# One written list of steps for the first attention, scores of two heads in one matmul, and weight conversion without GpSimd

## The chip, the cores and the metric

The kernel runs on one NeuronCore of one Trainium2 chip, in a single launch. A core has TensorE (PE in the profile; PEld is its weight load), VectorE (DVE), ScalarE (ACT), GpSimd (POOL) and SyncE (SP), each with an instruction queue of its own, and 16 DMA engines. The metric is device microseconds of one execution. Three runs of the kernel before took 930.74, 930.91 and 933.34 us; their median is 930.91 us.

## The reference

Two stages, for 8 batches of 576 rows. First an attention of 8 heads with 64 columns each, masked (heads 0 to 3 see the last 32 keys, heads 4 to 7 every 32nd key), then a mixing of rows and two large products:

```python
scores = scale * np.matmul(q, k.transpose(0, 1, 3, 2))
scores = np.where(masks[None, :, :, :], scores, -1000000000.0)
attn = np.exp(scores - np.max(scores, axis=-1, keepdims=True))
attn = attn / (np.sum(attn, axis=-1, keepdims=True) + 1e-09)
x = np.matmul(attn, v)            # heads side by side: (8, 576, 512)
h = x.transpose(0, 2, 1) @ U @ V  # U: 576 x 32, V: 32 x 576
u = x + h.transpose(0, 2, 1)
out = u + np.maximum(u @ w_ch1, 0.0) @ w_ch2   # 512 x 2048, 2048 x 512
```

q, k and v are float32; U, V, w_ch1 and w_ch2 come as float64, and the device turns them to float32 itself.

## The kernel before, in words

**Products.** The rows are cut into 9 blocks of 512 (8 batches' first 512 rows, and one block of what is left). For each block, `gemm1` makes 16 tiles of 128 hidden columns (12 matmuls each: 4 pieces of 128 inner rows, three products of high and low parts), and `gemm2` adds each into four accumulators (12 more). `gemm2` of a tile comes two tiles after its `gemm1` (`LAG`).

**Weights.** They arrive as 32 raw chunks of 128x512 float64, in the order of `CHUNK_SEQ`. `conversion` turns a chunk into high and low parts: two ACT instructions and two of DVE (`to_f32`), a copy on ACT into `parts[:, 0]`, and a subtraction on GpSimd (line 150) into `parts[:, 1]`. `gemm1` of the first tile needs the first four chunks.

**The first attention.** Batch 0 (strided heads as windows of reordered rows) is done before the first product. It is four pairs of heads: `scores` (two mask matmuls, then 36 small float32 ones, one for each 32 rows and head), `shifted` (maximum and subtraction on DVE), `exponentials` (ACT), `transposed` (five PE transposes), `to_sbuf` (ACT), `outputs` (36 small matmuls against the values and a column of ones), `normalised` (DVE). Then `mix_t` (x by U, for the strided and the local half), `u_strided_early` and `u_local` (transposes of x plus h, split into high and low parts `uh`, `ul`). The generators of the pairs are run three steps apart, and a scheduler that works with modelled times sets each engine's order there; the conversions of U, V and the first five chunks are held back behind an exponential by `gate`.

**The first block.** From the first product on, each engine's instructions stand in written order (`InOrder`). An agenda sets conversions, batch 1's attention ("second pairs") and the rest between halves of `gemm1` and `gemm2`, by ticks; 27 conversions start two ticks apart. In the later blocks the local heads go through `attention_pair`, and the strided heads of batches 2 to 7 run on GpSimd and DVE.

**DMA.** All transfers are issued by SP: keys, queries and values of pair 0, masks, the identity, pairs 2 and 3, U, V, pair 1, then 14 weight chunks.

All instructions of PE, DVE and ACT are issued in one helper, so they carry its line: L64 before and L69 after; DMAs are L86 and L92.

Of the kernel before, what the change touches and what calls it, by code (L numbers as in the profile page):

```python
# [19 lines left out]
NCH = S // 32  # L20
# [9 lines left out]
STAGGER = 3  # L30
ATT_BUFS = 7
PAIR_ORDER = (0, 2, 3, 1)
# [5 lines left out]
CHUNK_ORDER = (2, 3, 0, 1)  # L38


@with_exitstack
def fused_kernel(ctx, tc, lqk, lv, eqk, ev, sqkv, U, V, wts, masks, eye, out):
# [10 lines left out]
    class InOrder:  # L53
        on = False
# [15 lines left out]
    tensor, vector, scalar = InOrder(nc.tensor), InOrder(nc.vector), InOrder(nc.scalar)  # L70
# [12 lines left out]
    last_dma, gate, exps = [None], [], []  # L83

    def dma(out, in_):
        last_dma[0] = nc.sync.dma_start(out=out, in_=in_).ins  # L86
# [3 lines left out]
    masks_sb = const.tile([128, 768], BF16, name="masks_sb")  # L90
# [14 lines left out]
    def to_f32(raw, p, n, steps=1, gated=True):  # L105
# [5 lines left out]
        with tc.issue_after(gate[0]) if gated and gate else nullcontext():  # L111
            scalar.activation(out=f, in_=hi_w.bitcast(F32), func=AF.Abs, scale=2.0 ** -112)
            scalar.activation(out=low, in_=octet, func=AF.Copy, scale=1 / 32, bias=-15.5 / 32)
        yield steps
# [3 lines left out]
        vector.scalar_tensor_tensor(out=i, in0=i, scalar=3, in1=low, op0=ALU.logical_shift_left, op1=ALU.bitwise_or)  # L118
        yield steps
# [11 lines left out]
    def load_weights(n):  # L131
        while wl["loaded"] < min(n, len(chunks)):
            k = wl["loaded"]
            c = chunks[k]
            raws[c] = const.tile([128, 512], I64, name="raw%d_%d_%d" % c, tag=wtag(*c))
            with tc.issue_after(last_dma[0]):
                dma(out=raws[c], in_=wts[k])
            wl["loaded"] += 1

    def conversion(gated=False):  # L140
# [4 lines left out]
        f = yield from to_f32(raws[c], 128, 512, gated=gated)  # L145
        yield 1
# [3 lines left out]
        nc.gpsimd.tensor_tensor(out=parts[:, 1], in0=f, in1=parts[:, 0].bitcast(F32), op=ALU.subtract)  # L150

    def convert(n):
        while wl["conv"] < n:
            finished(conversion(True))
# [4 lines left out]
    raw_u = att([128, 320], "raw_u", I64)  # L159
    raw_v = ap_.tile([32, S], I64, name="raw_v", tag="vt")  # L160

    def small_loads():
        dma(out=raw_u, in_=U)
        dma(out=raw_v, in_=V)

    def small_u():
        f = finished(to_f32(raw_u, 128, 320))
        vector.tensor_copy(out=U_sb.rearrange("p v t r -> p (v t r)"), in_=f)

    def small_v():  # L170
        f = finished(to_f32(raw_v, 32, S))
        scalar.copy(out=Vst[0:32], in_=f)
        scalar.copy(out=Vst[32:64], in_=f)
        vector.tensor_tensor(out=Vst[64:96], in0=f, in1=Vst[0:32].bitcast(F32), op=ALU.subtract)
        nc.gpsimd.tensor_copy(out=Vp.rearrange("p (r i) -> p r i", i=NCH),
                              in_=Vst.bitcast(F32).rearrange("p (i r) -> p r i", r=32))
# [16 lines left out]

    def shifted(sp):
# [7 lines left out]
    def exponentials(s_sb):  # L202
        exped = scalar.activation(out=s_sb, in_=s_sb, func=AF.Exp, scale=0.125)
        if banks["prefix"]:
            exps.append(exped.ins)
            gate[:] = [exped.ins]
# [14 lines left out]
    def outputs(PT, vt):  # L221
        op = psx2()
        for c in range(NCH):
            t, c4 = c // 4, c % 4
            for hh, rows in enumerate(halves):
                tensor.matmul(op[32 * c4:32 * c4 + 32, hh, (D + 1) * t:(D + 1) * t + D + 1], PT[rows, 32 * c:32 * c + 32],
                                 vt(c)[rows], start=True, stop=True, skip_group_check=True,
# [3 lines left out]
    def normalised(op, pr):  # L231
        rt = ap_.tile([128, 16], F32, name="rt", bufs=2)[:, 0:10].rearrange("p (h t) -> p h t", h=2)
        for rows, ts in ((slice(0, 128), slice(0, 4)), (slice(0, 64), slice(4, 5))):
            o, r = op[rows, :, ts], rt[rows, :, ts]
            vector.tensor_scalar(out=r, in0=o[..., D], scalar1=1e-9, scalar2=None, op0=ALU.add)
            vector.reciprocal(out=r, in_=r)
# [125 lines left out]
    def mix_steps(b, half):  # L362
# [5 lines left out]
        for j in range(4):  # L368
            part = slice(64 * j, 64 * j + 64)
            tensor.matmul(ps_a[32 * j:32 * j + 32, part], U_sb[:, uv, 4, :], x[:, 4, part], start=False, stop=True,  # L370
# [12 lines left out]
        copied = scalar.copy(out=dst[64:96], in_=ta)  # L383
        if banks["prefix"]:
            gate[:] = [copied.ins]
        yield 1
        vector.tensor_tensor(out=dst[32:64], in0=ta, in1=dst[0:32].bitcast(F32), op=ALU.subtract)
# [12 lines left out]
    def split_steps(n, dcs, src, engine, order=None):  # L400
# [3 lines left out]
        scalar.copy(out=uh, in_=src)  # L404
        yield 1
# [17 lines left out]
    def u_local_steps(b, dcs):  # L423
        px = psx2()
        for dc in dcs:
            ps = px[:, dc % 2]
            for t in range(4):
                tensor.matmul(ps[:, 128 * t:128 * t + 128], x_loc[:, t, 128 * dc:128 * dc + 128], ident,
                                 is_transpose=True, start=t == 0, stop=False, skip_group_check=True)
            mixed(ps, b, dc, Vst, 0, TB, False)  # L430
# [15 lines left out]
    def u_strided_early_steps(b, dc):  # L446
        px = psx2().rearrange("p a x -> p (a x)")
        for t in range(5):
# [3 lines left out]
                             start=t in (0, 4), stop=False, skip_group_check=True)  # L452
        mixed(px[:, 0:512], b, dc, Vp, 0, 512, False)
# [3 lines left out]
        scalar.copy(out=tail_of(b)[:, dc].rearrange("p (i r) -> p r i", r=32), in_=src[:, :, 16:NCH])  # L457
        yield from split_steps(b, dc, src[:, :, 0:16], vector, "p (i r) -> p r i")
# [137 lines left out]
    def first_attention():  # L596
        late = [const.tile([128, 9, D + 1], F32, name=f"ve{n}", tag=wtag(n // 4, 3, n % 4)) for n in range(8)]
        loads = {}

        def load(k):  # L600
            pr = PAIR_ORDER[k]
            if k < 3:
                qk = places[2 * k:2 * k + 2]
            else:
                qk = [att([128, S], "kT"), att([128, S], "qT")]
# [33 lines left out]
        for dc in range(2):  # L639
            u_local(0, (dc,))  # L640
# [237 lines left out]
```

## Time and profile before

| what | value |
|---|---|
| three runs, median | 930.91 us (930.74 to 933.34) |
| the profiled execution's own time | 935.21 us |
| its span, first to last instruction | 933.4 us |
| PE busy, share of the span | 911.4 us, 98% |
| DVE, ACT, POOL busy | 531.4, 264.1, 406.2 us |
| first matmul of the attention | 7.47 us after the span's start |
| first matmul of the products | 44.74 us |

The profile has a page of sums, and a trace that can be asked for groups, waits and timelines. In a timeline, a row is start and length in us, engine, line, operation, what is written from what, and the shape; "x72" says how many equal ones are merged, and the brackets tell the idle time before and what ended it. The length of a matmul is the time until its modelled end, so matmuls that follow each other overlap; the distance of their starts tells the rate. Times within the span are counted from its start. The profiled execution took 4.3 us more than the median of the three runs.

### The profile page before, as it was taken

How to read it: one execution, taken by the hardware profiler on the slowest of the kernel's cores; microseconds unless marked ns; L12 is line 12 of the kernel's file. 1: busy time of each engine (PE TensorE's matmuls, PEld its weight loads, DVE VectorE, ACT ScalarE, POOL GpSimd, SP SyncE). 2: the span in 40 equal slices, each digit the busy share in tenths (PEclk: the TensorE clock that was granted, in tenths of full speed). 3: DMA queues.
4: the chain of work that ended last, by engine and by line, in shares of the span. 5: the costliest groups of instructions: out<-in, count | busy, mean ns of one | idle time of the engine just before them, and what ended most of it. 6: DMA issues, size and time to landing. Idle time of an engine off the chain costs nothing.

```text
span 933.4 us, 16532 instructions
## 1 busy us (share of the span) xinstructions
PE 911.4 (98%) x6896; PEld 724.7 (78%) x6896; DVE 531.4 (57%) x878; ACT 264.1 (28%) x520; POOL 406.2 (44%) x407
## 2 busy tenths in 40 slices
PE   5799999999999999999999999999999999999998
PEld 3567777778778877787877787787788788888886
DVE  3777885659465965488457936594659631112112
ACT  2666763114311241115111411142112421111110
POOL 0143345839185726754475629391948220002000
PEclk9979999999999999999999999999999999999999
DMA  9990031120222012111111022202210030001001
GB/s 343 405 370 28 27 101 34 46 78 1 59 94 61 19 51 91 38 52 52 58 72 53 2 81 72 78 1 76 78 52 1 1 97 1 0 1 46 1 1 45
DMA packets 27098, 64.50 MB, mean 69 GB/s; under 512 B 6768, under 2 KB 7280, under 8 KB 27024
## 3 DMA queue, kind: packets, MB, share of 16 engines
q1 hardware_dynamic: 27024, 63.45, 19.6%
q8 instruction: 54, 0.88, 0.4%
q14 instruction: 20, 0.16, 0.1%
HBM read 52.96 MB, written 10.49 MB: 68 GB/s over the span
## 4 chain that ended last, share of the span: by engine, by line
PE 92%; issue 3%; DVE 2%; ACT 1%; POOL 1%; DMA 1%; SPq 0%; DVEq 0%; POOLq 0%; ACTq 0%
PE acc L64 42%; PE ph L64 42%; PE px L64 8%; POOL w L150 1%; DVE cv L64 1%; DMA masks_sb<-in_masks_dram 1%; ACT raw L64 0%; ACT cv L64 0%; DVE raw L64 0%; SPq L86 0%; ACT s_sb L64 0%; DVE ta L64 0%; DVE o L64 0%; ACT PT L64 0%; DVE mx L64 0%
## 5 line engine op out<-in xcount | busy, mean ns | idle before, releaser
L64 PE MATMUL ph<-uh,w 128*128 128x512 f32 x1152 | 386.5, 396 | 2.1 <-ACT w L64 1.1
L64 PE MATMUL acc<-gh,w 128*128 128x512 f32 x1152 | 387.8, 393 | 0.6 <-DVE o L64 0.4
L64 DVE SCALAR_TENSOR_TENSOR gl<-ph,gh 128x512 fp32r<-128x512 f32 x144 | 99.2, 689 | 306.0 <-ACT gh L64 306.0
L64 PEld LDWEIGHTS ph<-uh,w 128*128 128x128 f32 x1152 | 218.1, 190 | 50.5 <-ACT w L64 1.8
L64 PEld LDWEIGHTS acc<-gh,w 128*128 128x128 f32 x1152 | 215.3, 188 | 48.6 <-issue 2.5
L64 PE MATMUL ph<-ul,w 128*128 128x512 f32 x576 | 227.4, 395 | 0.1
L64 PE MATMUL acc<-gl,w 128*128 128x512 f32 x576 | 226.0, 392 | 0.0
L64 ACT ACTIVATE gh<-ph 128x512 fp32r<-128x512 f32 x144 | 86.0, 597 | 452.0 <-PE ph L64 445.9
L308 POOL TENSOR_TENSOR tmp<-st,st 128x576 f32<-128x576 f32 (+6 forms) x162 | 167.1, 1066 | 82.6 <-DMA st<-in_sqkv_dram 36.9
L334 POOL TENSOR_TENSOR tmp<-st,s_st 128x448 f32<-128x448 f32 (+7 forms) x162 | 135.5, 875 | 56.3 <-DVE s_st L64 56.3
L64 DVE TENSOR_REDUCE st<-tmp 128x64 f32<-128x64 f32 (+8 forms) x162 | 132.6, 886 | 0.2
L64 PEld LDWEIGHTS ph<-ul,w 128*128 128x128 f32 x576 | 109.2, 190 | 23.2 <-DVE ul L64 0.4
L64 PEld LDWEIGHTS acc<-gl,w 128*128 128x128 f32 x576 | 108.2, 188 | 22.7
L64 DVE TENSOR_REDUCE s_st<-tmp 128x9 f32<-128x576 f32 (+6 forms) x162 | 87.9, 567 | 24.8 <-POOL tmp L308 21.8
L561 POOL TENSOR_TENSOR o<-o,uh 128x512 f32<-128x512 f32 x32 | 40.5, 1288 | 103.2 <-DVE o L64 103.2
L150 POOL TENSOR_TENSOR w<-cv,w 128x512 fp32r<-128x512 f32 x32 | 45.3, 1419 | 75.9 <-ACT w L64 73.4
L64 ACT COPY x_str<-st 32x256 f32<-32x256 f32 (+1 forms) x144 | 50.5, 351 | 33.7 <-DVE st L64 32.2
L406 POOL TENSOR_TENSOR ul<-st,uh 128x1024 fp32r<-128x1024 f32 x6 | 14.4, 2400 | 103.1 <-ACT uh L64 103.1
L64 DVE SCALAR_TENSOR_TENSOR cv<-cv,raw 128x512 int32<-128x512 int32 x32 | 34.3, 1070 | 2.3
L64 ACT ACTIVATE s_sb<-s_sb 128x640 f32<-128x640 f32 x20 | 14.8, 739 | 68.8 <-DVE s_sb L64 68.8
L64 DVE SCALAR_TENSOR_TENSOR raw<-raw 128x512 int32<-128x512 int32 x32 | 24.9, 779 | 9.3 <-ACT raw L64 9.3
L64 ACT CAST w<-cv 128x512 fp32r<-128x512 f32 x32 | 19.6, 617 | 9.0 <-DVE cv L64 7.8
(103 smaller groups left out, 486.1 us busy)
## 6 DMA issues: line engine op xcount, KB each, us to landing
raw<-in_wts_dram SPq DMA_DIRECT2D x32, 512.0 KB, 9.8
st<-in_sqkv_dram SPq DMA_DIRECT2D x18, 576.0 KB, 4.2
out_dram<-o SPq DMA_DIRECT2D x35, 256.0 KB, 2.0
vt<-in_lv_dram SPq DMA_DIRECT2D x14, 585.0 KB, 3.9
kT<-in_lqk_dram SPq DMA_DIRECT2D x13, 288.0 KB, 3.0
qT<-in_lqk_dram SPq DMA_DIRECT2D x13, 288.0 KB, 4.0
scr<-in_eqk_dram SPq DMA_DIRECT2D x8, 288.0 KB, 6.9
scr<-in_lqk_dram SPq DMA_DIRECT2D x6, 288.0 KB, 6.8
```

The costliest lines, as they stand in the source:

```text
L64: r = op(*args, **kwargs)
L150: nc.gpsimd.tensor_tensor(out=parts[:, 1], in0=f, in1=parts[:, 0].bitcast(F32), op=ALU.subtract)
L308: nc.gpsimd.tensor_tensor(out=tmp[:, 0:n], in0=sk[:, j0:j0 + n], in1=sq[:, i:i + 1].broadcast_to([128, n, D]), op=ALU.mult)
L334: nc.gpsimd.tensor_tensor(out=tv, in0=sv[:, 0:i + 1, d0:d0 + step], in1=s_st[:, i, 0:i + 1].broadcast_to([128, i + 1, step]), op=ALU.mult)
L406: engine.tensor_tensor(out=ul, in0=src, in1=uh.bitcast(F32), op=ALU.subtract)
L561: nc.gpsimd.tensor_tensor(out=o, in0=o, in1=uh[:, m].bitcast(F32), op=ALU.add)
```

## The change

It touches the part up to the first product, and the conversions after it.

- `InOrder` is on from the start: the order of PE, DVE, ACT and GpSimd is the written list `FIRST` (f8: eight matmuls of ones that nobody reads; S scores, M `shifted`, E exponentials, T transposes, P copy, O outputs, N `normalised` of one pair; w0 to w4 the next step of a chunk's conversion; U, V their conversions; tS, tL0, tL1 mixing; uS, uL the sums). Transfers go in the order of `LOADS`.
- `both_scores`: the keys of two heads are loaded into one tile with zeros between (rows 0 to 63: head one's keys, then zeros; rows 64 to 127: zeros, then head two's), so one matmul of 128 rows and 128 columns does what two of 64 rows and 64 columns did. 18 instead of 36 for a pair. Zeros are written by DVE and GpSimd once.
- `outputs` in this part first writes 1e-9 into the sum's column by two matmuls (`eps`), so that `normalised` needs no addition and takes all rows at once.
- `mix_direct` instead of `mix_steps` in this part: five matmuls, one after another, into 32 PSUM rows, so that no sum over four groups of rows is needed; the local half is done in two halves of columns.
- The low parts of the weights are subtracted on DVE, in all 32 conversions; V comes three times from DRAM; the cast of `Vp` moves from GpSimd to ACT. In the first block the conversions start up to two ticks sooner.

```diff
-PAIR_ORDER = (0, 2, 3, 1)
+PAIR_ORDER = (2, 3, 0, 1)
+FIRST = """
+f8 V V V S1 V S0 M1 V S2 M0 E1 w0 T1 M2 E0 P1 T0 w0 E2 S3 w0 P0 w0 O1 M3 U T2 N1 E3 O0 P2 U w1 T3 N0 w2 w1 tS P3 w2 w1
+O2 tS w1 w2 tS uS0 w3 N2 uS0 w2 uS1 uS0 w3 uS1 O3 uS1 uS0 tL0 w4 N3 uL0 uS1 tL1 tL0 w3 tL0 uL1 w4 tL1 uL0 uL0 tL1 w4
+w3 uL1 uL1 uL0 uL1 w4
+""".split()
+LOADS = "V masks k1 k0 k2 c0 ident k3 v1 U v0 c1 c2 c3 v2 c4 v3".split()
...
     class InOrder:
-        on = False
+        on = True
...
-    def conversion(gated=False):
+    def conversion():
...
         scalar.copy(out=parts[:, 0], in_=f)
-        nc.gpsimd.tensor_tensor(out=parts[:, 1], in0=f, in1=parts[:, 0].bitcast(F32), op=ALU.subtract)
+        yield 1
+        vector.tensor_tensor(out=parts[:, 1], in0=f, in1=parts[:, 0].bitcast(F32), op=ALU.subtract)
...
+    def both_scores(keys, qT, mask):
+        sp = psx2().rearrange("p a x -> p (a x)")
+        m = mask.rearrange("p (t x) -> p t x", x=64)[:, :, None, :]
+        for t0, t1 in ((0, 4), (4, 5)):
+            tensor.matmul(sp[:, 128 * t0:128 * t1].rearrange("p (t h x) -> p t h x", h=2, x=64), ident_b,
+                          m[:, t0:t1].broadcast_to([128, t1 - t0, 2, 64]), start=True, stop=False, skip_group_check=True)
+        for c in range(NCH):
+            t, c4 = c // 4, c % 4
+            x0 = 0 if c else 32
+            out = sp[32 * c4:32 * c4 + 32, 128 * t:128 * t + 128].rearrange("p (h x) -> p h x", h=2)[:, :, x0:64]
+            tensor.matmul(out, qT[:, 32 * c:32 * c + 32], keys(c), start=False, stop=True, skip_group_check=True,
+                          tile_position=(0, 32 * c4))
+        return sp[:, 0:640].rearrange("p (t h x) -> p h t x", h=2, x=64)
...
     def outputs(PT, vt):
         op = psx2()
+        if banks["prefix"]:
+            for hh in range(2):
+                tensor.matmul(op[:, hh, 0:5 * (D + 1)], warm_w[0:96], eps.broadcast_to([96, 5, D + 1]), start=True, stop=False,
+                              skip_group_check=True)
...
+    def mix_direct(b, half, cols):
+        x, uv = (x_str, 1 if b < NSP else 0) if half else (x_loc, 0)
+        ps = ps_h.tile([128, 512], F32, name="ph")[0:32, cols]
+        for j in range(5):
+            rows = slice(0, 128 if j < 4 else 64)
+            tensor.matmul(ps, U_sb[rows, uv, j, :], x[rows, j, cols], start=j == 0, stop=j == 4)
+        yield 1
+        if b not in tsts:
+            tsts[b] = ap_.tile([96, DM], F32R, name="tst")
+        dst = tsts[b][:, 256 * half + cols.start:256 * half + cols.stop]
+        scalar.copy(out=dst[0:32], in_=ps)
+        scalar.copy(out=dst[32:64], in_=ps)
+        yield 1
+        vector.tensor_tensor(out=dst[64:96], in0=ps, in1=dst[0:32].bitcast(F32), op=ALU.subtract)
...
+        def fill(n):
+            for _ in range(n):
+                tensor.matmul(idle, warm_w, warm_w[:, None, :].broadcast_to([128, 4, 128]), start=True, stop=True)
...
-            agenda_add(conversion(), 2 * k)
+            agenda_add(conversion(), max(0, 2 * k - 2))
```

How the instructions stand on the engines, at three places. First, PE where the first pair's scores stand and what comes around them; `acc` and `px` are PSUM tiles, `scr`, `kd` and `qd` hold keys and queries. Before (the third pair's scores, then the second pair's transposes and outputs):

```order
L64 LDWEIGHTS masks_sb
L64 MATMUL acc<-masks_sb 128x320
L64 MATMUL acc<-scr 32x32 x2
L64 MATMUL acc<-scr 32x64 x34
L64 MATMUL px<-ident,s_sb 128x128 x4
L64 MATMUL px<-ident,s_sb 128x64
L64 MATMUL acc<-ve_92,PT 32x65 x18
L64 MATMUL acc<-ve_93,PT 32x65 x18
```

and now, from the last of eight matmuls of ones on (`warm_w`):

```order
L69 LDWEIGHTS warm_w
L69 MATMUL ph<-warm_w 128x512
L69 LDWEIGHTS masks_sb
L69 MATMUL acc<-masks_sb 128x512
L69 LDWEIGHTS masks_sb
L69 MATMUL acc<-masks_sb 128x128
L69 MATMUL acc<-scr 32x2x32
L69 MATMUL acc<-scr 32x128 x17
```

Eight matmuls of ones now stand ahead of everything; a pair's scores are 18 matmuls of 128 columns instead of 36 of 64, and three pairs' scores stand behind one another before the first transposes.

Second, PE between the last attention outputs and the first product; `Vst` and `Vp` are V, `tst` is x by U. Before:

```order
L64 MATMUL px<-ve_97,PT 32x65 x18
L64 MATMUL acc<-x_str,U_sb 32x256 x4
L64 MATMUL acc<-x_str,U_sb 32x64 x4
L64 MATMUL acc<-ident,x_str 128x128 x4
L64 MATMUL acc<-ident,x_str 128x64
L64 MATMUL px<-x_loc,U_sb 32x256 x4
L64 MATMUL px<-x_loc,U_sb 32x64 x4
```

and now:

```order
L69 LDWEIGHTS warm_w
L69 MATMUL acc<-masks_sb,warm_w 128x325
L69 MATMUL acc<-ve_97,PT 32x65 x18
L69 MATMUL acc<-ve_98,PT 32x65 x18
L69 MATMUL ph<-x_loc,U_sb 32x128 x5
L69 MATMUL px<-ident,x_loc 128x128 x4
L69 MATMUL ph<-x_loc,U_sb 32x128 x5
L69 MATMUL acc<-ident,x_loc 128x128 x4
L69 MATMUL px<-Vst,tst 128x512
```

The rows of the strided half (`ph<-x_str,U_sb 32x256 x5`) now stand before the outputs of the third pair; each mixing is five matmuls into the same 32 rows where it was four side by side and four short ones.

Third, DVE in the first block, between two `gl` (the low part of a hidden tile); `raw` and `cv` are a chunk's conversion, `mx` and `s_sb` a second pair's scores. Before:

```order
L64 SCALAR_TENSOR_TENSOR gl<-ph,gh 128x512
L64 SCALAR_TENSOR_TENSOR raw_1_3_134<-raw_1_3_134 128x512
L64 SCALAR_TENSOR_TENSOR cv<-cv,raw_1_3_134 128x512
L64 TENSOR_REDUCE mx<-px 128x10
L64 TENSOR_TENSOR s_sb<-px,mx 128x2x5x64
L64 SCALAR_TENSOR_TENSOR gl<-ph,gh 128x512
```

and now:

```order
L69 SCALAR_TENSOR_TENSOR gl<-ph,gh 128x512
L69 SCALAR_TENSOR_TENSOR raw_1_0_158<-raw_1_0_158 128x512
L69 SCALAR_TENSOR_TENSOR cv<-cv,raw_1_0_158 128x512
L69 TENSOR_REDUCE mx<-px 128x10
L69 TENSOR_TENSOR s_sb<-px,mx 128x2x5x64
L69 TENSOR_TENSOR w_1_3_771<-cv,w_1_3_771 128x512
L69 SCALAR_TENSOR_TENSOR gl<-ph,gh 128x512
```

A chunk now takes three instructions of DVE instead of two, and the subtraction `w` stands in DVE's queue ahead of `gl`; before, it stood on GpSimd alone.

More of the change, by code (lines that the diff above doesn't have):

```diff
@@ L202, in exponentials @@
     def exponentials(s_sb):
[L203 to L206, printed above, removed]
+        scalar.activation(out=s_sb, in_=s_sb, func=AF.Exp, scale=0.125)
     def transposed(s_sb):
@@ L404, in split_steps @@
         scalar.copy(out=uh, in_=src)
+        if beside is not None:
+            beside()
         yield 1
@@ new lines, in window, with values @@
+        def window(k, c):
+            k0, k1 = max(0, 32 * c - 32), 32 * c + 32
+            if k < 3:
+                return wide[k][:, :, k0:k1]
+            z, s0 = (halves_k[0], 0) if c < 9 else (halves_k[1], 256)
+            return z[:, :, k0 - s0:k1 - s0]
+        def values(k):
+            pr = PAIR_ORDER[k]
+            src = lv[0, pr] if pr < 2 else ev[0, pr - 2]
+            for n in range(2):
+                dma(out=late[2 * k + n].rearrange("p c x -> p (c x)"), in_=src[:, 9 * (D + 1) * n:9 * (D + 1) * (n + 1)])
@@ new lines, in S_, with M, E, T @@
+        def S_(k):
+            pr = PAIR_ORDER[k]
+            sp[k] = both_scores(lambda c: window(k, c), q_places[k], masks_sb[:, 320 * (pr // 2):320 * (pr // 2) + 320])
+        def M(k):
+            s_sb[k] = shifted(sp[k])
+        def E(k):
+            exponentials(s_sb[k])
+        def T(k):
+            pp[k] = transposed(s_sb[k])
+        def P(k):
+            PT[k] = to_sbuf(pp[k])
+        def O(k):
+            op[k] = outputs(PT[k], lambda c: late[2 * k + c // 9][:, c % 9])
+        def N(k):
+            normalised(op[k], PAIR_ORDER[k])
@@ new lines, in first_attention @@
+        gens = {}
+        pool.memset(warm_w, 1.0)
+        for n, z in enumerate(wide + halves_k):
+            for hh, rows in enumerate(halves):
+                (vector if n < 2 else pool).memset(z[rows, 1 - hh], 0.0)
+        small = {"masks": (masks_sb, masks), "U": (raw_u, U), "V": (raw_v, V), "ident": (ident, eye)}
+        for name in LOADS:
+            if name in small:
+                dma(*small[name])
+            else:
+                {"k": keys, "v": values, "c": lambda k: load_weights(k + 1)}[name[0]](int(name[1:]))
@@ L643, in fused_kernel @@
+        for name in FIRST:
+            if name in gens:
+                next(gens[name], None)
+            else:
+                steps[name[0]](int(name[1:]))
     first_attention()
@@ L814, in _masks @@
                 m[32 * c4 + qq, 1, t] = np.where(strided, 0.0, 8.0 * NEG)
-    return np.concatenate([m.reshape(128, 640), np.eye(128, dtype=m.dtype)], axis=1)
+    eps, rest = np.zeros((128, D + 1), m.dtype), 1e-9
+    for row in (0, 32, 64):
+        eps[row, D] = rest
+        rest -= float(eps[row, D])
+    return np.concatenate([m.reshape(128, 640), np.eye(128, dtype=m.dtype), eps], axis=1)
 def _layouts(q, k, v, U, V, w1, w2):
```

150 lines of the change are left out of this document (68 added, 82 removed).

## The prediction

> **What bounds the kernel now.** The page came first: its busy times, and PE's line over 40 slices.
>
> ```profile
> PE 911.4 (98%) x6896; PEld 724.7 (78%) x6896; DVE 531.4 (57%) x878; ACT 264.1 (28%) x520; POOL 406.2 (44%) x407
> PE   5799999999999999999999999999999999999998
> ```
>
> PE is full from the third slice on, so time can only be won before about 62 us, or lost by opening a gap later. Next, busy time by stretch: the attention up to the first product (7 to 45 us), the first products, one stretch of the first block.
>
> ```profile
> 7.00:45.00 38.00, 29.31 (x661) 19.91 (x662) 23.95 (x57) 17.83 (x33) 4.07 (x3) 1.00 1.03 399
> 45.00:62.30 17.30, 15.15 (x109) 9.84 (x108) 12.48 (x16) 10.66 (x20) 6.77 (x5) 0.70 1.03 408
> 60.00:120.00 60.00, 59.81 (x685) 45.86 (x685) 48.90 (x73) 39.77 (x72) 23.17 (x17) 0.99 0.23 85
> ```
>
> After the length come PE, PEld, DVE, ACT and POOL, then the granted clock. Of the first 38 us PE works 29.3. What it waits for up to 45 us:
>
> ```profile
> PE acc L64 <- DMA masks_sb<-in_masks_dram: 7.5, 1, 7.5
> PE acc L64 <- ACT PT L64: 2.2, 3, 0.8
> PE acc L64 <- issue: 2.1, 2, 1.1
> PE px L64 <- ACT PT L64: 1.9, 1, 1.9
> PE acc L64 <- DVE ul L64: 0.8, 1, 0.8
> PE px L64 <- ACT s_sb L64: 0.7, 1, 0.7
> PE px L64 <- issue: 0.5, 1, 0.5
> ```
>
> So 5.6 us go to ACT and DVE, 2.6 to "issue", and the rest of the attention is PE's own work. How fast that work runs is what decides here:
>
> ```profile
> 24.29 1.41 PE L64 MATMUL px<-ident,s_sb 128*128 128x128 f32 x5
> 44.74 0.63 PE L64 MATMUL ph<-uh,w 128*128 128x512 f32 x1
> 45.17 0.63 PE L64 MATMUL ph<-ul,w 128*128 128x512 f32 x1
> 46.87 0.63 PE L64 MATMUL ph<-uh,w 128*128 128x512 f32 x1
> 48.56 0.50 PE L64 MATMUL ph<-uh,w 128*128 128x512 f32 x1 [1.06 <-ACT w L64]
> 51.60 1.22 PE L64 MATMUL ph<-uh,w 128*128 128x512 f32 x2 [0.72 <-POOL w L150]
> 62.60 0.39 PE L64 MATMUL ph<-ul,w 128*128 128x512 f32 x1
> 62.84 0.39 PE L64 MATMUL ph<-uh,w 128*128 128x512 f32 x1
> 67.85 0.80 PE L64 MATMUL px<-ident,s_sb 128*128 128x128 f32 x5
> 47.40:50.80 3.40, 1.98 (x6) 0.86 (x5) 3.01 (x5) 1.93 (x5) 2.22 (x2) 1.00 1.03 404
> 50.00:51.00 1.00, 0.88 (x3) 0.40 (x3) 0.41 (x1) 0.50 (x1) 1.00 (x1) 0.92 1.05 402
> 61.00:62.00 1.00, 1.00 (x66) 0.74 (x68) 0.97 (x2) 0.00 (x0) 1.00 (x1) 0.96 1.02 406
> ```
>
> The clock column reads 1.00 before 47 us, but it only repeats the lack of a record: five transposes take 1.41 us there and 0.80 at 67.85, and products start 0.43 us apart at 44.74 and 0.23 at 62.6. **The whole attention runs at half clock.** The clock rises between 46.87 and 48.56, falls at 50.84 (0.92 of a microsecond's mean) and rises again at 61.08 (0.96): 10.24 us at half rate, three times 3.41, and 3.41 before 50.84 is 47.43. So I take a gate that decides every 3.41 us. In the window that ended at 47.43 products streamed nine tenths of the time, and it rose. In the next, five products of 0.21 us (x6 with the end of the one at 46.87), 31%, and it fell. In 50.84 to 54.25 products started at 51.6 and streamed some 75%, and it did not rise. Raising thus needs between 75 and 92%; a share that falls lies at 31% or above.
>
> **The change part by part,** against the point where before starts its first product after a second pair's scores, 62.27 us; from there both programs give PE the same work. Rows for the prices at half clock:
>
> ```profile
> 7.47 0.72 PE L64 MATMUL acc<-masks_sb 128*128 128x320 bf16 x2 [7.47 <-DMA masks_sb<-in_masks_dram]
> 14.11 1.69 PE L64 MATMUL acc<-ve,PT 64*32 64x65 f32 x72 [0.73 <-ACT PT L64]
> 15.74 0.72 PE L64 MATMUL acc<-masks_sb 128*128 128x320 bf16 x2
> 16.38 1.31 PE L64 MATMUL acc<-scr 64*32 64x32 f32 x72
> 17.62 1.41 PE L64 MATMUL px<-ident,s_sb 128*128 128x128 f32 x5
> 37.23 1.29 PE L64 MATMUL px<-x_loc,U_sb 128*32 128x256 f32 x16
> 37.66 0.20 PEld L64 LDWEIGHTS px<-x_loc,U_sb 128*32 128x32 f32 x4 [0.23 <-issue]
> 38.09 0.20 PEld L64 LDWEIGHTS px<-x_loc,U_sb 128*32 128x32 f32 x4 [0.23 <-issue]
> q8 instruction: 54, 0.88, 0.4%
> ```
>
> Scores: 36 matmuls are 72 passes, so float32 takes two. Masks 0.64 (15.74 to 16.38), scores 1.24 (to 17.62). Now 18 matmuls are 36 passes of 128 columns, four side by side: nine rounds. A round of 256 columns takes 0.43 (37.66 to 38.09), so these take 0.21 each, 1.92, plus the 0.28 that before has over its nine rounds of 0.107: 2.20. Fewer instructions, 0.96 us more of the array, four times 3.8; the first pair's masks are done before its keys land, so +3.2. If issuing bound it, 36 passes would cost 0.6: with the rounds seen in both rows I keep 2.20.
>
> Outputs: 650 columns of bf16 ahead, as the masks' 640: 0.64 each, +2.6. Mixing: ten passes into the same 32 rows cannot run side by side: 4.3 us for 256 columns, twice 2.1 for the halves, 8.5 instead of twice 1.29: +5.9. What it saves, a copy and three additions, lay behind other work except the 0.8 us wait for `ul`. Groups that stood alone have a tail of 0.2 (a 0.11 pass is shown as 0.31) that dense work covers: about -1.2. PE's work: 29.0 (up to 44.74) + 3.2 + 2.6 + 5.9 - 1.2 = 39.5 us at half clock.
>
> Issue: 54 fetches for 13,792 instructions of PE are 255 each, and stalls of 0.5 to 1.1 lie about that far apart. 288 fewer for the scores, some 30 more elsewhere: one fetch less; 2.1 us kept, 0.8 to 3.3.
>
> Start: the first scores need 1216 KB (V, masks, one pair's queries and keys); before, 1353 KB had landed at 7.43. So 7.0, give or take 0.5. The eight matmuls of ones (3.4 us) fit ahead of it and cost nothing; at best they raise the clock for one window.
>
> Waits: with three pairs' scores in a row PE has other work wherever it waited 5.6 us, so none at half clock, up to 2.8 at most. For nothing I count, behind this PE work: the `Vp` cast on ACT ahead of the first exponential (1 us if uncovered), the zeros, the shorter `normalised`, and 0.3 MB more of DMA (0.8 us at 400 GB/s) before chunks that are converted later than they land.
>
> First product, clock down throughout: 7.0 + 39.5 + 2.1 = 48.6, where before has 44.74. But before then loses the time to 62.27: products wait for chunks not yet converted, and for the clock. Now five chunks are ready. 30 products lie there, 12 until the clock rises (5.1 us, one to two windows) and 18 at 0.23 (4.1), `u_tail` 0.4, second scores 1.27 (61.00 to 62.27 as follows): 10.9.
>
> ```profile
> 61.00 0.48 PE L64 MATMUL px<-masks_sb 128*128 128x320 bf16 x2
> 62.27 0.50 PE L64 MATMUL ph<-uh,w 128*128 128x512 f32 x1
> ```
>
> That gives 59.5, 2.8 less than 62.27. The sum is made against the profiled execution's 935.21 us: **932.4**. The median of the runs is 930.91; 23 products at half clock after 47.43 cost at most 4.6, so runs without that fall explain the difference.
>
> **How far the clock comes up** is the open term. A pair's scores now stream 0.53 + 1.92 of 2.85 us, 86%, three in a row; a mixing streams always, on a quarter of the columns. Both are in the gap from 75 to 92%. Outputs (70%) and transposes with waits (about half) lie between 31 and 75, where falling is open. So likeliest it rises in some windows and falls in others: half of the 39.5 us at full clock saves a quarter, 9.9, and half of the 5.6 of waits comes back: first product at 41.5, and 52.4 instead of 62.27: 9.9 less, **925.3**.
>
> **Rivals.** (1) The clock stays down until the products: 932.4, within the bound of the median. For it: no window of before's attention raised it, with PE busy in 77% of the time. (2) It comes up early and stays: 7.0 + 19.8 + 2.1 + 5.6 = 34.5, then 30 products at 0.23, 0.4 and 1.27: 43.1, 19.2 less, 916.0. For it: no window is empty any more. Against it: the fall after a window at 31%. The Trainium skill, "TensorE: Matmul & The Clock Gate", Part 1, has windows of about 3.4 us, a rise after a busy one and a fall after an idle one; the trace agrees in the length, but the window that fell here was not idle. (3) Slower: DVE, not PE, bounds the first block. Rows between 60 and 120 us, and one pair of an instruction under POOL's subtraction and one beside none:
>
> ```profile
> L64 DVE SCALAR_TENSOR_TENSOR cv<-cv,raw 128x512 int32<-128x512 int32 x17 | 19.1, 1124 | 1.4
> L64 DVE SCALAR_TENSOR_TENSOR raw<-raw 128x512 int32<-128x512 int32 x17 | 12.9, 758 | 4.4 <-ACT raw L64 4.4
> 30.49 0.69 DVE L64 SCALAR_TENSOR_TENSOR cv<-cv,raw 128x512 int32<-128x512 int32 x1
> 55.22 1.27 POOL L150 TENSOR_TENSOR w<-cv,w 128x512 fp32r<-128x512 f32 x1 [2.43 <-DMA raw<-in_wts_dram]
> 55.38 1.66 DVE L64 SCALAR_TENSOR_TENSOR cv<-cv,raw 128x512 int32<-128x512 int32 x1
> ```
>
> A chunk costs DVE 1.88 now and three times 0.69, 2.07, with GpSimd silent: 17 x 0.19 = 3.2 on 48.9 of 60 us, 87%, and PE never waits. If the two stay at 1.88, the subtraction adds 17 x 0.69 = 11.7: 60.6 of 60. Then `gl` and the chunks behind it are late, PE waits 1 us in that stretch, and from a wait that empties two thirds of a window the clock falls for 10.24 us (4.6 each). Two falls: 925.3 + 1 + 9.2 = 935.5. Against it, the 0.69 beside an idle POOL.
>
> **How the numbers follow.** Clock in part 0.43 (own range 920 to 930), clock down 0.27, clock up 0.20, DVE-bound 0.10. No change is what lies within 0.3%, 928.1 to 933.7, about what this measurement can tell. Faster: 0.20 + 0.39 + 0.03 = 0.62; same: 0.04 + 0.20 + 0.03 = 0.27; slower: 0.04 (clock down with the stalls at 3.3 and waits at 2.8) + 0.07 = 0.11. The range runs from 913 (clock up, start and stalls at their lower ends) to 932.5 (clock down).
>
> **What would show it.** Transposes at 0.8 instead of 1.4 us between 10 and 45 us show the clock up, and how long; a first product near 41 the likeliest case, 48 or 35 the rivals; a pair's scores at 2.2 us (1.1 at full clock) and mixing at 4.3 or 2.1 the prices; no PE wait between first product and second scores the prepared chunks; `cv` and `raw` at 0.69 the quiet port. I am wrong if the clock follows another rule than the share of streaming, or if PE waits for ACT and DVE in spite of three pairs in flight.

## The result, and the profile after

The changed kernel takes 918.05 us (median of four runs, 917.0 to 920.69); the kernel before took 932.12 us beside it (930.74 to 934.62). The ratio is 0.985, with a 95% interval from 0.9818 to 0.9883: 1.5% faster, with the whole interval below 1. The forecast was 925.3 us. The range from 913 to 932.5 holds the time, the likeliest case's own range from 920 to 930 does not; the nearest case is the second rival, the clock that comes up early and stays (916.0).

The profiled execution after took 917.0 us with a span of 915.2; before it was 935.21 and 933.4. That is 18.2 us, more than the 14.1 between the medians, because the profiled execution of before lay 3.1 us above its median and that of after 1.05 below. All marks inside the span are compared with each other, and all verdicts with the medians.

The busy times on the page of after:

```profile
PE 905.3 (99%) x6766; PEld 719.5 (79%) x6766; DVE 532.0 (58%) x889; ACT 264.2 (29%) x520; POOL 363.7 (40%) x380
```

PE has 130 matmuls, as many weight loads and 6.1 us of busy time less, and 9.9 of its 22 idle us (the span less its busy time) are left. Busy time after in the stretches that the prediction showed of before (length, PE, PEld, DVE, ACT, POOL, granted clock, DMA share, GB/s):

```profile
7.00:45.00 38.00, 35.12 (x631) 24.66 (x632) 32.73 (x55) 28.80 (x53) 1.40 (x1) 0.96 1.04 379
45.00:62.30 17.30, 17.30 (x214) 13.61 (x213) 15.47 (x29) 12.92 (x23) 0.00 (x0) 1.00 1.03 406
60.00:120.00 60.00, 60.00 (x632) 46.31 (x633) 52.35 (x99) 40.98 (x75) 0.02 (x1) 1.00 0.37 135
```

TensorE works in 35.1 of the 38 us up to 45, where it had 29.3. From 60 us on nothing is won or lost: it is full, and VectorE's 52.35 of 60 us are the 87% that the prediction worked out. What TensorE waits for up to 45 us:

```profile
PE acc L69 <- DMA scr<-in_eqk_dram: 2.3, 1, 2.3
...
PE ph L69 <- DVE x_str L69: 0.9, 1, 0.9
PE acc L69 <- ACT s_sb L69: 0.6, 1, 0.6
...
PE acc L69 <- issue: 0.3, 1, 0.3
```

Instead of 5.6 us for ACT and DVE and 2.6 for "issue" there are some 2 and 0.3. The 2.3 us stand before the first scores. Rows of TensorE's timeline after:

```profile
7.65 2.21 PE L69 MATMUL acc<-scr 128*32 128x64 f32 x36 [2.33 <-DMA scr<-in_eqk_dram]
9.79 0.71 PE L69 MATMUL acc<-masks_sb 128*128 128x512 bf16 x2
...
12.41 1.28 PE L69 MATMUL px<-kd,qd 128*32 128x64 f32 x36
13.63 0.86 PE L69 MATMUL acc<-ident,s_sb 128*128 128x128 f32 x5
...
22.94 2.46 PE L69 MATMUL ph<-x_str,U_sb 128*32 128x256 f32 x10 [0.86 <-DVE x_str L69]
...
35.55 0.40 PE L69 MATMUL ph<-uh,w 128*128 128x512 f32 x1
...
44.31 0.50 PE L69 MATMUL ph<-uh,w 128*128 128x512 f32 x1
```

The first pair's scores take 2.14 us (7.65 to 9.79), the third's 1.22 (12.41 to 13.63), five transposes 0.86 instead of 1.41: full clock from about 11 us on. The first product comes at 35.55 (44.74 before), the first one after the second scores at 44.31 (62.27). So 17.96 of the span's 18.2 us are won by then, about half before the first product (9.2) and half behind it (8.8).

The trace's clock records say up at 4.43, down at 7.85, and up from 11.26 us to the end. Busy time in the gate's own windows of 3.41 us (columns as above: PE first, the granted clock after POOL):

```profile
1.02:4.43 3.41, 3.41 (x8) 1.01 (x8) 2.05 (x4) 1.04 (x2) 2.38 (x6) 1.00 0.78 226
4.43:7.85 3.42, 0.79 (x12) 0.34 (x15) 1.51 (x2) 1.81 (x3) 0.00 (x0) 1.00 1.04 279
7.85:11.26 3.41, 3.41 (x55) 2.44 (x50) 1.33 (x2) 1.32 (x2) 1.40 (x1) 0.50 1.05 264
...
21.50:24.91 3.41, 2.55 (x14) 1.20 (x13) 3.28 (x7) 3.21 (x6) 0.00 (x0) 1.00 1.03 401
```

The 1.00 of the first window only repeats the lack of a record, as in the kernel before: the fill's eight matmuls start 0.43 us apart there, the distance at half clock. The fill's full window raises the clock and so does that of the scores, the window with 0.79 us of work lets it fall, and the emptiest one after 11.26, with 2.55 of 3.41 us, keeps it. Not every full window raises it: in the kernel before, these two came at half clock, the first with mixing and transposes, the second with products and a few small matmuls, and the clock stayed down after both.

```profile
37.19:40.61 3.42, 3.42 (x25) 2.20 (x25) 2.29 (x6) 1.17 (x3) 0.00 (x0) 1.00 1.04 408
54.26:57.67 3.41, 3.41 (x11) 2.28 (x10) 2.74 (x3) 0.89 (x2) 1.27 (x1) 0.50 1.04 416
```

So a busy TensorE is not the whole rule of the rise; what else it takes stays open.

### The profile page after: what moved, and what is told of

Read it like the earlier page. It is cut to its first block, busy times and chain, and to the rows that moved or that the text cites. A ratio compares the mean times of both kernels' runs of the same rounds, so it can differ in the third digit from the quotient of the medians.

```text
span 915.2 us, 16178 instructions
## 1 busy us (share of the span) xinstructions
PE 905.3 (99%) x6766; PEld 719.5 (79%) x6766; DVE 532.0 (58%) x889; ACT 264.2 (29%) x520; POOL 363.7 (40%) x380
## 4 chain that ended last, share of the span: by engine, by line
PE 97%; DVE 1%; DMA 1%; issue 0%; SPq 0%; ACT 0%; DVEq 0%; ACTq 0%
PE acc L69 45%; PE ph L69 44%; PE px L69 8%; DMA scr<-in_eqk_dram 1%; DVE mx L69 0%; SPq L92 0%; DVE s_sb L69 0%; DVE raw L69 0%; DVE cv L69 0%; DVE o L69 0%; DVE x_str L69 0%; DVE ul L69 0%; DVE x_loc L69 0%; DVE w L69 0%; ACT w L69 0%
## 5 line engine op out<-in xcount | busy, mean ns | idle before, releaser
L69 PE MATMUL ph<-uh,w 128*128 128x512 f32 x1152 | 382.1, 392 | 0.0
L69 PEld LDWEIGHTS ph<-uh,w 128*128 128x128 f32 x1152 | 215.9, 188 | 45.9
L69 PE MATMUL ph<-ul,w 128*128 128x512 f32 x576 | 225.1, 391 | 0.0
L69 DVE SCALAR_TENSOR_TENSOR raw<-raw 128x512 int32<-128x512 int32 x32 | 22.0, 688 | 3.5 <-ACT raw L69 3.4
L69 DVE SCALAR_TENSOR_TENSOR cv<-cv,raw 128x512 int32<-128x512 int32 x32 | 22.2, 693 | 1.1
L69 DVE TENSOR_TENSOR w<-cv,w 128x512 fp32r<-128x512 f32 x32 | 21.8, 685 | 0.8 <-ACT w L69 0.7
L69 DVE TENSOR_TENSOR o<-acc,ul 128x512 f32<-128x512 f32 x32 | 20.6, 684 | 2.4 <-DMA out_dram<-o 2.1
```

The source lines that it names most:

```text
L69: r = op(*args, **kwargs)
```

## The experiments

### Fewer instructions, or more streaming?

The zeros make a pair's scores both shorter in instructions and longer in the array. The first of two runs undoes both, the second the number of instructions alone. First, scores of one head at a time from the same tiles, in the same written list (twice the instructions, half the columns):

```diff
-            sp[k] = both_scores(lambda c: window(k, c), q_places[k], ...)
+            sp[k] = scores_by_head(lambda c: window(k, c), q_places[k], ...)
+            # as `scores`: 2 masks, then 36 of qT[rows, 32 * c:32 * c + 32] by keys(c)[rows, hh], 64 rows each
```

> The changed kernel with the scores of one head at a time, as before: 36 matmuls of 64 rows from the same tiles with zeros between, the written list and all else kept. Theory (the zeros' matmuls raise the clock, since they stream 2.2 us of work for 1.24): a window of scores has too little streaming, the clock stays down for most of the attention: first product at 45 to 48 us, 928 to 932 us. Rival (the order does it: three pairs' scores in a row without a wait are dense enough in either form): the clock rises at about 11 us too and a pair's scores at full clock take 0.95 instead of 1.22 us: 916.5 to 918.5.

924.50 us, ratio 0.9917 (0.9892 to 0.9942). Neither expectation: half of the gain stays. Rows of its timeline:

```profile
15.53 0.44 PE L69 MATMUL px<-kd,qd 64*32 64x64 f32 x8 [3.24 <-issue]
...
24.24 0.68 PE L69 MATMUL acc<-ve,PT 64*32 64x65 f32 x40 [2.55 <-issue]
```

and three of the gate's windows by busy time:

```profile
11.21:14.62 3.41, 1.08 (x65) 0.81 (x64) 1.20 (x2) 2.27 (x4) 0.00 (x0) 1.00 1.05 348
21.45:24.86 3.41, 0.86 (x69) 0.63 (x49) 0.82 (x1) 0.74 (x1) 0.00 (x0) 1.00 1.02 403
24.86:28.28 3.42, 3.42 (x82) 2.27 (x81) 2.02 (x6) 1.93 (x4) 0.00 (x0) 0.50 1.05 414
```

The clock rises at 11.2 us in this form too. But then TensorE stands 3.24 and 2.55 us with nothing that the profile knows to wait for, these two windows are largely empty (1.08 and 0.86 of 3.41 us), and the clock falls after each (down from 14.62 to 21.44 and from 24.86 to 28.27). Each time a fetch of instructions lands 1.4 us before work goes on: in the trace's records of the instruction queue one ends at 14.12 and one at 22.81 us.

Second, the same columns with the same zeros, but each matmul cut into its two heads:

```diff
-            tensor.matmul(out, qT[:, 32 * c:32 * c + 32], keys(c), ...)
+            for hh in range(2):
+                tensor.matmul(out[:, hh], qT[:, 32 * c:32 * c + 32], keys(c)[:, hh], ...)
```

> The changed kernel with each of the 18 score matmuls of a pair cut into two of 64 columns: the same columns through the array with the same zeros, but as many instructions as one head at a time. Theory 1 (instructions: one head at a time lost 3.24 and 2.55 us at 15.5 and 24.2 us in which TensorE had nothing to run until a fetch of instructions landed, and the clock fell in these windows): the same stalls come here, together 4 to 6 us, the clock falls at least once after 11 us, 922 to 926 us. Theory 2 (streaming: the zeros' columns keep the clock up, however they are cut): no more than 0.5 us of stalls, clock up from 11.3 us, 917 to 919.5 us.

924.58 us, ratio 0.9914 (0.9893 to 0.9936): theory 1. Its timeline:

```profile
15.53 0.42 PE L69 MATMUL px<-kd,qd 128*32 128x64 f32 x8 [1.44 <-issue]
...
24.21 0.94 PE L69 MATMUL acc<-ve,PT 64*32 64x65 f32 x40 [3.99 <-issue]
```

The stalls stand before the same instructions as in the run before, with other streaming; the clock is down from 23.1 to 29.9 us. So it is the number of TensorE's instructions that costs 6.4 us here, and the columns of zeros alone do nothing for it. Two things make up the loss, the stalls themselves (3.24 and 2.55 us, here 1.44 and 3.99) and the stretches at half clock behind them (6.8 and 3.4 us, here 6.8); what each of them costs was not tried apart.

### How fast instructions come

In the kernel before, the three stalls on "issue" had stood at equal distances:

```profile
21.80 0.68 PE L64 MATMUL acc<-ve,PT 64*32 64x65 f32 x28 [1.10 <-issue]
...
28.11 1.10 PE L64 MATMUL acc<-ve,PT 64*32 64x65 f32 x53 [0.98 <-issue]
...
34.31 0.42 PE L64 MATMUL px<-ve,PT 64*32 64x65 f32 x3 [0.52 <-issue]
```

They end 6.31 and 6.20 us apart. Two kernels measure this pace by itself: 1200 pairs of a weight load and a tiny matmul ahead of everything, once with all loads held behind them, once without (one execution each, 952.14 and 958.23 us; only their first 45 us matter here).

```diff
         pool.memset(warm_w, 1.0)
+        for n in range(1200):
+            c4 = n % 4
+            tensor.matmul(idle[32 * c4:32 * c4 + 32, 0, 0:32], warm_w[:, 0:32], warm_w[:, 0:32], ..., tile_position=(0, 32 * c4))
+        seen = ap_.tile([32, 8], F32, name="seen", bufs=1)              # these three: held only
+        scalar.copy(out=seen, in_=idle[96:128, 0, 0:8])
+        dma(out=dram.tile([32, 8], F32, name="held"), in_=seen)
```

> The changed kernel with 1200 tiny matmuls (a weight load and a matmul of 32 columns each, 2400 instructions, nobody reads what they write but one small copy) ahead of everything, and all loads held until they are done, so that TensorE's instructions are fetched while no other transfer runs. With the transfers at 400 GB/s, fetches of 255 instructions began 6.1 to 6.4 us apart at the closest, and TensorE stood up to 3.99 us. Theory (a fetch is slow because it stands behind the transfers): here nine fetches follow 1 to 3 us apart and stand at most 1 us in all. Rival (a fetch comes every 6 us at best, whatever else moves): they begin about 6 us apart, the 2400 instructions take 50 us or more, and TensorE stands before each. The whole time is the changed kernel's plus that stretch, 945 to 980 us, and says nothing by itself.

Held, the timeline:

```profile
0.99 2.02 PE L69 MATMUL ph<-warm_w 128*32 128x32 bf16 x223 [0.99 <-POOL warm_w L69]
5.24 1.23 PE L69 MATMUL ph<-warm_w 128*32 128x32 bf16 x128 [2.23 <-issue]
8.69 1.23 PE L69 MATMUL ph<-warm_w 128*32 128x32 bf16 x128 [2.23 <-issue]
12.42 1.23 PE L69 MATMUL ph<-warm_w 128*32 128x32 bf16 x128 [2.50 <-issue]
```

A stretch of it by busy time (the last column is GB/s):

```profile
10.00:15.00 5.00, 1.23 (x128) 1.13 (x128) 0.00 (x0) 0.00 (x0) 0.00 (x0) 1.00 0.01 3
```

And the page's row of the instruction queue (transfers, MB, share of the DMA engines):

```profile
q8 instruction: 62, 1.02, 0.5%
```

223 pairs, 446 instructions, run at once; then 128 pairs, 256 instructions, at a time, 3.45 to 4.0 us apart, with a stall of 2.2 to 2.8 us before each, while the transfers move 3 GB/s. Neither expectation is right: a fetch (1.02 MB in 62, 16 KB each) has a pace of its own, but a quicker one than 6 us.

> The same 1200 tiny matmuls ahead of the changed kernel, but the loads are not held: keys, values and 14 chunks arrive at up to 400 GB/s while TensorE runs them. With the loads held, fetches of 256 instructions followed 3.46 to 3.91 us apart and TensorE stood 2.23 to 2.78 us before each. Theory (a fetch has a pace of its own, and the transfers beside it make it slower): 6 to 7 us apart and stalls of 4.5 to 6 us each while transfers run, the last tiny matmul at 50 to 65 instead of 31.4 us. Rival (the pace is the same, and the 6.1 to 6.4 us seen in the attention are how fast TensorE used its instructions there): 3.5 to 4 us apart here too, the last one at about 32 us.

Not held, four rows of the timeline:

```profile
21.90 1.23 PE L69 MATMUL ph<-warm_w 128*32 128x32 bf16 x128 [3.88 <-issue]
27.83 1.22 PE L69 MATMUL ph<-warm_w 128*32 128x32 bf16 x128 [4.70 <-issue]
34.02 1.23 PE L69 MATMUL ph<-warm_w 128*32 128x32 bf16 x128 [4.97 <-issue]
40.22 1.23 PE L69 MATMUL ph<-warm_w 128*32 128x32 bf16 x128 [4.97 <-issue]
```

and a stretch by busy time:

```profile
25.00:30.00 5.00, 1.22 (x128) 1.12 (x128) 0.00 (x0) 0.00 (x0) 0.00 (x0) 1.00 1.03 402
```

Beside 390 to 410 GB/s the groups are 5.9 to 6.2 us apart and the stalls up to 4.97; earlier in this run, beside 260 to 280 GB/s, they were 4.3 to 5.7 us apart. So the theory holds in its direction, with a pace at the lower end of its 6 to 7 us: TensorE gets some 74 instructions per us when nothing else moves (256 / 3.45), 41 beside full transfers (256 / 6.2). The attention runs beside full transfers nearly all the time. The fetch's own packet takes 0.9 to 1.6 us in either run, so most of the pace is not its data; what it is was not seen.

The Trainium skill, "Runtime: NRT & Kernel Launch", section "Instruction fetch mechanics", has blocks of 16 KiB (256 instructions) that are fetched while earlier ones run, at a cost that is mostly hidden. The trace agrees in the 256 and the 16 KB; the cost is hidden here only where 256 instructions last longer than the pace above, as in the products, where from 60 to 120 us no stall on instructions is left.

One more run tried to ease the queue in the attention itself:

```diff
-        load_weights(14)
+        def H(k):                    # a step of the list, behind P2
+            dma(out=dram.tile([1, 8], F32, name="held"), in_=PT[k][0:1, 0:8])
+            load_weights(14)
```

> One head at a time in the changed kernel, as the run before, but the loads of the weights' chunks from the sixth on start only when the third pair's transposes are copied (a small transfer that reads them stands ahead in the queue), so that the queue is empty from about 20 us until then. One head at a time lost 3.24 us without instructions before 15.5 us, while transfers ran at 400 GB/s, and 2.55 before 24.2. Theory (a fetch of instructions is slow because it stands behind the transfers): the first stall stays at 3 us, the second is below 1 us, the clock doesn't fall at 24.9 us: first product at 38 to 40 instead of 41.8 us, and 920 to 923 us if the later chunks are still in time (up to 3 more if not). Rival (a fetch takes 6 us or more of its own): the second stall stays at 2 to 3 us and the time at 924 or above.

923.90 us, ratio 0.9906 (0.9885 to 0.9927), stalls of 3.34 and 3.21 us. It tells nothing: the transfers still ran at 396 GB/s between 22 and 24 us, since what stood ahead of the hold landed until 29.3 us. The two kernels above answer the question instead.

### The clock without the list, and the list with other fills

The kernel before with a fill that raises the clock, alone and with the zeros' scores (the tiles and loads of the changed kernel, before's own order):

```diff
+        for _ in range(18):
+            tensor.matmul(idle, warm_w, warm_w[:, None, :].broadcast_to([128, 4, 128]), start=True, stop=True)
         load(0)
         dma(out=masks_sb, in_=masks)
...
-        sp = scores(kT, qT, mask)                                             # in the second of the two runs
+        sp = both_scores(kT, qT, mask) if callable(kT) else scores(kT, qT, mask)
```

> The kernel before with 18 matmuls of ones ahead of its first masks, where TensorE waits 7.5 us; its order is otherwise the same. Theory (the clock is the gain): if the attention keeps the clock that the fill raises, its 29 us of work at half clock shrink by up to 14, what is given back is at most the waits for ACT, DVE and instructions (about 5), and the fall at 50.8 us goes or stays (5): 916 to 926 us. Rival (the list and the five chunks that stand ready are the gain): whatever the clock does, products wait for chunks between 35 and 62 us: 929 to 933 us. If the clock falls in the attention's first gap in spite of the fill, the run says only that before's order doesn't hold it: 930 to 935.

931.57 us, ratio 0.9994 (0.9979 to 1.0008): no change, though the clock was up from 4.33 to 14.57 us. What the faster attention had won by then it gave back at once, as this row of its timeline shows:

```profile
16.68 0.65 PE L64 MATMUL acc<-ve,PT 64*32 64x65 f32 x22 [3.04 <-issue]
```

At half clock it had used its instructions about as fast as they came; at full clock it stands 3.04 us (13.64 to 16.68), and the clock falls meanwhile, at 14.57, and stays down until 55.53. By its expectation the run says only that before's order does not hold the clock.

> The kernel before, in its own order, with two parts: the zeros' scores of two heads in one matmul for batch 0 (288 instructions of TensorE fewer), and 18 matmuls of ones ahead of the first masks. The fill alone raised the clock for 10.24 us, TensorE then stood 3.04 us without instructions at 13.6 us, the clock fell, and the time did not change. Theory 1 (instructions): without that stall the clock stays up past 14.6 us, at least until the waits of 2 us between 30 and 34; first product at 36 to 42 instead of 46.9 us, 920 to 927 us. Theory 2 (before's order loses the clock anyway, by its waits for ScalarE between a pair's steps): the clock falls by 18 us, first product at 44 to 47, 929 to 933 us.

930.25 us, ratio 0.9978 (0.9964 to 0.9992). No stall on instructions is left, and the clock stays up from 7.53 to 28.01 us, as theory 1 has it. But the time is that of theory 2, because before's order runs into ACT and DVE. Three rows of its timeline:

```profile
26.47 0.97 PE L64 MATMUL acc<-ve,PT 64*32 64x65 f32 x72 [3.02 <-DVE x_str L64]
28.80 1.41 PE L64 MATMUL acc<-ident,s_sb 128*128 128x128 f32 x5 [1.35 <-ACT s_sb L64]
32.60 1.37 PE L64 MATMUL px<-ve,PT 64*32 64x65 f32 x72 [2.40 <-ACT PT L64]
```

The waits leave 0.97 us of work in the window from 24.59 to 28.01, and the clock falls. (The zeros and the fill also put the first scores at 9.88 instead of 8.12 us.) So fewer instructions are worth 1.3 us in before's order, where the two runs' intervals overlap, and in the written list 6.4.

The list with no fill and with a longer one:

```diff
-f8 V V V S1 V S0 M1 ...
+V V V S1 V S0 M1 ...             # no fill
+f18 V V V S1 V S0 M1 ...         # the other run
```

> The changed kernel without its eight matmuls of ones at the start, nothing else. In the changed kernel the clock rose at 4.43 us after them, fell at 7.85 after a window with little but masks in it, and rose for good at 11.26 after the window of the first two pairs' scores. Theory (the scores of three pairs in a row raise the clock and the later work keeps it): the fill gives nothing, first product at 35 to 37 us, 917 to 921 us. Rival (the fill is needed, it sets where the gate's windows lie or counts for the rise at 11.26): the clock rises one or more windows later, each at 1.7 us, or not before the mixing, and then 925 to 932 us.

> The changed kernel with 18 matmuls of ones instead of eight, so that TensorE streams until the first keys arrive at 7.65 us. Theory (a window with some 50% of streaming keeps the clock): the clock stays up from 4.4 us, the scores of the first two pairs take 1.22 instead of 2.14 us each, 1.8 us less: 915.5 to 917. Rival (it falls in that window anyway): 917.5 to 920, no change; where the gate's first decision comes late, the fill runs into the scores' time and costs up to 1.5 us.

917.61 us, ratio 0.9841 (0.9821 to 0.9862), and 916.82 us, 0.9831 (0.9811 to 0.9851). Without a fill the clock rises at 11.10, by the scores: the eight matmuls of ones do nothing. With 18 it is up from 5.97, both first pairs run at full clock, and the first product comes at 34.82 instead of 35.55. This is the lowest time of all; it lies 1.2 us below the changed kernel, where 1.8 were expected, but within the intervals.

### The other parts

The subtraction on GpSimd again (`pool.tensor_tensor` for `vector.tensor_tensor` in `conversion`):

> The changed kernel with the low part of the weights subtracted by GpSimd again, in all 32 conversions, the list otherwise kept. Theory (the clock makes the gain): the five chunks ahead of the first product come at most 1 to 2 us later and cv and raw go back from 0.69 to about 1.0 us on VectorE, which has 13% to spare in the first block: 917.5 to 920 us. Rival (the quiet port is a good part of the gain): VectorE falls behind with the chunks, TensorE waits for w in the first block, 922 to 930 us.

918.58 us, ratio 0.9855 (0.983 to 0.988): no difference to the changed kernel. The groups of the two kernels between 60 and 120 us (last the busy time and the mean in ns); the changed kernel:

```profile
L69 DVE SCALAR_TENSOR_TENSOR cv<-cv,raw 128x512 int32<-128x512 int32 x17 | 11.8, 693 | 0.6
```

and with the subtraction on GpSimd:

```profile
L69 POOL TENSOR_TENSOR w<-cv,w 128x512 fp32r<-128x512 f32 x18 | 25.2, 1400 | 38.5 <-ACT w L69 38.5
L69 DVE SCALAR_TENSOR_TENSOR cv<-cv,raw 128x512 int32<-128x512 int32 x18 | 18.9, 1048 | 1.5
```

VectorE's instruction is 0.36 us slower beside GpSimd, as predicted, but neither form holds TensorE up there.

The outputs without the two matmuls of 1e-9, and the mixing with four groups of rows as before:

```diff
-            for hh in range(2):
-                tensor.matmul(op[:, hh, 0:5 * (D + 1)], warm_w[0:96], eps.broadcast_to([96, 5, D + 1]), ...)
+            vector.tensor_scalar(out=r, in0=o[..., D], scalar1=1e-9, scalar2=None, op0=ALU.add)   # 128 rows, then 64
...
-        gens["tS"] = mix_direct(0, 1, slice(0, 256))                      # the other run; tL0 and tL1 likewise
+        gens["tS"], gens["tL0"] = mix_steps(0, 1), mix_steps(0, 0)    # and the list's steps to match
```

> The changed kernel without the two matmuls that put 1e-9 into the sums of a pair's outputs; the addition is done on VectorE again, for 128 and 64 rows apart, as before. Theory (price at full clock, from the profile of the changed kernel: 0.39 us of TensorE each pair, and VectorE has no room there, where TensorE waited 0.86 us for x_str): 1.6 us less on TensorE, some 0.7 us more VectorE in each of the four pairs, most of it in front of that wait: 917 to 919 us, no change. Rival (they are pure work on the path, as I priced them): 916 to 917 us. If the matmuls are needed to keep the clock, it falls and the time is 920 or more.

> The changed kernel with the mixing as before, four groups of rows side by side and the sum of the four on VectorE, in the written list (the local half in one piece again, behind the third pair's last step). Theory (price at full clock: TensorE 2.39 and 2 times 1.32 us now, 0.65 each then, 3.7 us less, but a copy and three additions of 0.4 us more stand between the mixing and the transposed sums that wait for it, twice 1.7 us, and the local half waits for the last pair): what TensorE saves it waits: 917 to 920 us. Rival (TensorE's work decides, as I priced it): 914 to 915.5 us. If the gap empties half a window, the clock falls: 921 to 925 us.

919.36 us, ratio 0.9866 (0.9846 to 0.9887), and 923.66 us, 0.992 (0.9891 to 0.9949). Less work on TensorE makes neither faster. The second is clearly slower; the first lies 1.3 us above the changed kernel, which the intervals do not tell apart, though in its profiled execution the first product comes at 37.29 instead of 35.55. Without the 1e-9 matmuls, the row of the mixing:

```profile
23.31 2.25 PE L69 MATMUL ph<-x_str,U_sb 128*32 128x256 f32 x9 [1.62 <-DVE rt L69]
```

and the window around it:

```profile
21.77:25.19 3.42, 1.88 (x12) 0.83 (x14) 3.25 (x12) 2.34 (x5) 0.00 (x0) 1.00 1.02 397
```

The wait before the mixing grows from 0.86 to 1.62 us: VectorE is busy in 3.25 of 3.42 us there, so that what is moved to it delays the mixing. With the four groups (the local half is then in one piece again, behind the third pair's last step), two rows of the timeline:

```profile
34.60 1.45 PE L69 MATMUL acc<-x_loc,U_sb 128*32 128x256 f32 x16 [1.14 <-DVE ul L69]
...
38.87 0.77 PE L69 MATMUL acc<-Vst,tst 96*128 96x512 f32 x1 [1.78 <-DVE tst L69]
```

and the window in which the clock is lost:

```profile
21.88:25.29 3.41, 2.12 (x62) 1.00 (x70) 3.31 (x7) 3.10 (x6) 0.00 (x0) 1.00 1.02 396
```

The shorter mixing leaves TensorE 2.12 us of work in the window from 21.88, the clock falls at 25.3 and is down until 42.36, and the later waits for VectorE come on top: 5.6 us. The window after next, 28.71 to 32.12, is full (3.41 of 3.41 us) and does not raise it.

## Why the prediction was right and wrong

**How far the clock comes up** is the step that failed. The prediction took "half of the 39.5 us at full clock" as likeliest, from the shares of streaming of single windows. Measured, all work from 11.26 us on ran at full clock, and so did the first products. Of the 8.1 us between its 52.4 and the measured 44.31, 5.95 lie ahead of the first product (41.5 and 35.55) and 2.1 behind it (10.9 and 8.76), where it had 12 products at half clock. Its reading of the gate was right in part: windows of 3.41 us, and full windows of scores raise it; that two full windows of the kernel before, shown above, did not raise it, it left out. But what makes it fall was looked for in the kind of work (outputs, transposes), and it lies in gaps. Of all windows in these runs that began at full clock in the attention, those with up to 1.73 us of TensorE's work let it fall and those from 2.2 up kept it; between 1.88 and 2.12 both happened (1.88, 1.97 and 2.08 kept it, 1.99 and 2.12 did not), so this measure gives no sharp limit. The Trainium skill, "TensorE: Matmul & The Clock Gate", Part 1, lets it fall after an idle window; by the trace a window was idle enough with 1.73 of its 3.41 us busy.

**Issue: "one fetch less; 2.1 us kept"** is the step behind it. The prediction counted the fetches (rightly: the page after has 53) and took the stalls as a fixed cost of each. They are what is missing when 256 instructions last less than a fetch, 6.2 us here, and the distances of before's three stalls (6.31 and 6.20) had shown that pace. So it missed two things: with twice the work to an instruction of the scores the stalls nearly vanish (0.29 us), and with by-head scores the faster clock makes its own stall and falls again. That self-limit is what held half the gain back in the by-head run. In the kernel before with a fill it ended the full clock, but it is not the only limit there: without any such stall the time was 930.25 all the same.

**The prices** were near where a row had given them, and mostly too low: a pair's scores 2.14 (2.20) and 1.22 at full clock (1.1), the mixing 2.39 and twice 1.32 at full clock (2.15 and twice 1.05), the first scores at 7.65 (7.0, give or take 0.5). PE's work at full clock was sized too low: 35.55 - 7.65 - 2.2 of waits is 25.7 us, of which 3.6 at half clock, so about 23.9 at full clock, where the second rival had 19.8. That it came within 1.1 us of the first product (34.5 for 35.55) was luck: its stalls and waits (2.1 and 5.6) were 5.5 us too high together, which made up for most of 4.1 of work, 1.8 for the half clock until 11.26 and 0.65 at the start.

**The sign of the mixing** was wrong. It was priced at +5.9 us, with what it saves "behind other work", and it is a gain: 5.6 us are lost without it, since what it saves lies on VectorE, for which TensorE then waits, and since TensorE's shorter work leaves a window empty enough for the clock to fall. The 1e-9 matmuls, priced at +2.6, cost nothing that could be measured: without them the time was 1.3 us longer, within the intervals.

**Waits.** "None at half clock" could not be seen; at full clock 1.9 us were left for ACT and DVE, a third of the 5.6 that the second rival kept. That part of the gain goes with the list: the by-head kernel, with the list, won 7.3 us, and the kernel before with fewer instructions and a fill only 1.3. The list was not tried without the change's other parts, such as the mixing.

**Between first product and second scores** the 30 products, with `u_tail` and the scores, took 8.76 us (8.6 in the second rival's sum) and had no wait for chunks. That half of the gain, 8.8 us, the by-head run has too (41.83 to 50.60), so the score matmuls have no part in it. The list with its prepared chunks is the likely cause, but what of it is the missing waits and what the clock that does not fall there was not tried apart.

**VectorE as the bound** (third rival): 0.69 us for `cv` and `raw` beside an idle GpSimd and 87% busy, both as worked out; the first block never waits. The subtraction's place makes no difference to the time. The first rival (clock down until the products, 932.4) was refuted by the trace.

## What to carry to other kernels

Many small matmuls in a row can run out of instructions: compare the time that 256 of them take with the distance of the stalls marked "issue" in the profile, and make fewer and larger ones, with zeros in them if need be, before trying to make them faster. A stretch at half clock costs nearly half of its length (products start 0.43 us apart there and 0.23 at full clock), so ask of each change which windows of 3.4 us it leaves half empty: more work on TensorE that takes a step off a full VectorE can win twice, as the mixing did here.

## What the runs showed of the hardware

- TensorE starts with 446 instructions at hand, then gets 256 at a time: 3.45 to 4.0 us apart with no other transfers, 5.9 to 6.2 us beside 390 to 410 GB/s, up to 4.97 us of them standing still.
- The clock and this pace work against each other: the kernel before used its instructions at half clock about as fast as they came, and a fill that doubled the clock for 10 us changed its time by nothing (0.9994).
- The gate falls after windows that are not idle at all: 2.12 of 3.41 us busy was too little in one run, 1.88 enough in another.
- At half clock, a window that the profile shows full does not always raise the clock: two in the kernel before (37.19 to 40.61 and 54.26 to 57.67 us) and one in the run with four groups (28.71 to 32.12) did not.
